# Weight conversion steps at the banks ahead of the seven-product pairs of a fused retention and two-MLP kernel: one per bank in place of two

## The chip, the cores and the metric

The kernel runs on one core of one Trainium2 chip. The metric is the device time of one execution in microseconds (us), the median of several runs. Engines are named as in the profile: PE is the matrix engine, DVE the vector engine, ACT the scalar engine, POOL and SP the two that here mostly issue transfers.

## The reference, cut to what matters

```python
def _attn_ref(q, k, v, lam):              # B=2, H=8, S=768, D=64; block 64
    ...                                   # decayed (retention) attention, a running 64x64 state per head
def _moe_ref(x, w_in, w_out):
    h = np.maximum(x @ w_in, 0.0)         # 512 -> 2048
    return (h * h @ w_out)                # 2048 -> 512
def _moe2_ref(x, w_in, w_out):
    h = x @ w_in
    g = np.maximum(0.01 * h, h)
    return (g @ w_out)
def reference(**kwargs):
    attn_out = _attn_ref(**attn_kwargs)
    x = attn_out.transpose(0, 2, 1, 3).reshape(B * S, H * D)   # 1536 x 512
    return _moe2_ref(_moe_ref(x))
```

The four weight matrices arrive as 64-bit words.

## The kernel before

First comes the retention (`retention`, one chunk of 128 tokens at a time), then two MLP layers. An MLP layer is cut into four stages by slices of 512 of the 2048 hidden columns; a stage is written (layer, slice), so the order is (0,0) ... (0,3), (1,0) ... (1,3). The 1536 tokens are three tiles of 512 (t = 0, 1, 2). In a stage, `first` multiplies the tokens by the slice of the first matrix: four banks (m = 0 to 3) a tile, each 12 matmuls of 128x512 in two halves of 6, and each half ends with a `yield`. `second` multiplies by the slice of the second matrix, again four banks of 12 matmuls. Values are split into a high and a low part, so one product takes three matmuls.

In stages (0,1) and (0,2), the set `seven`, tiles 0 and 1 of the second multiplication are done together by seven products in place of eight (`second_pair`, a Strassen form). Each of the 14 products (two output halves, p = 0 and 1) is 6 matmuls. They need sums of activations and sums of weights. `activate_for_seven` forms the former right behind each bank of `first`: for each half it chains L491 (a difference on DVE), L68 (a copy on ACT), L69 (the low part on DVE, T1), L449 to L451 (three more differences) and L69 again (T2), all with raised priority. The order of the products is P1 (A11 B11), S1 T1, A12 B21, S4 B22, S2 T2, A22 T4, then `first` of tile 2, then S3 T3.

The weights of later stages are prepared meanwhile. A piece is named (layer, slice, n, half), n = 0 for the first matrix and 1 for the second. `converting` is a generator that turns one piece of 64-bit words into floats and splits it; each `yield` is one step: L115, L116, L118, L121, L122 (then `fetch` issues the load of a later piece), L125, and, once the tile it goes to is open, L135 on ACT with L137 on DVE. L114 on ACT comes ahead of L115. A second-matrix piece of the `seven` stages has three more steps with the weight sums (`weight_sums`: L437 and L438; L439 and L440; L441 on ACT and L442). `convert` takes the next step of the oldest unfinished piece, at most two (of some kinds four) being open. The loop at the end of the kernel calls `convert` once behind every `yield` that is not False.

The order on PE is that of the program. On DVE, ACT, SP and POOL a scheduler sets the order ahead of time: where several instructions are ready, the one emitted earlier in the program goes first (L490, L495 and the like raise some by 400 places). So a call of `convert` sets where its step is emitted, which is a precedence and not a time. Working buffers limit how far ahead a piece can get: two for the raw words (`raw`), two for `hb` (pieces that `apart` names have their own), and one for `rb`, which L121 to L125 use and, for the pieces of `seven`, L437 to L442 in a tile of its own.

The steps of the prediction touch `first` (L505 to L525), `convert` (L153), `converting` (L98), `second_pair` (L620), and `keep` (L610), which copies a finished product (L612, ACT) to one of nine `f` tiles and writes it out from SP (partials) or adds it in memory from POOL (L616).

Of the kernel before, what the change touches and what calls it, by code (L numbers as in the profile page):

```python
# [19 lines left out]
def tile_retention_then_two_mlps(  # L20
# [37 lines left out]
    def bank():  # L58
        return psum.tile([P, 512], F32, tag="ps", name="ps")

    def plain():
        return fp.tile([P, TT], F32, tag="f", name="f")
# [110 lines left out]
    seven = {(0, 1), (0, 2)}  # L173
# [250 lines left out]
    def new_g(t, first_stage=False):  # L424
        if first_stage and t == 2:
            tags = ("sw0", "sw1")
        else:
            tags = (f"g{t % 2}h", f"g{t % 2}l")
        g[t] = [late.tile([P, KF, TT], F32R, tag=tag, name=tag) for tag in tags]
# [36 lines left out]
    def activate(l, src, r, ghi, glo):  # L466
        if l == 0:
            nc.scalar.activation(r, src, AF.Relu)
            nc.scalar.square(ghi, r)
            nc.scalar.square(r, r)  # L470
        else:
            nc.scalar.activation(ghi, src, AF.Prelu, alpha=0.01)
            nc.scalar.activation(r, src, AF.Prelu, alpha=0.01)
        nc.vector.tensor_tensor(out=glo, in0=r, in1=ghi, op=ALU.subtract)  # L474
# [4 lines left out]
    def activate_for_seven(t, m, src):  # L479
        r = plain()  # L480
        later[t, m] = r
        nc.scalar.activation(r, src, AF.Relu)
        ghi, glo = g[t]
        if (t, m % 2) != (1, 0):
            nc.scalar.square(ghi[:, m], r)
        nc.scalar.square(r, r)
        if (t, m % 2) != (1, 0):
            nc.vector.tensor_tensor(out=glo[:, m], in0=r, in1=ghi[:, m], op=ALU.subtract)
        if (t, m % 2) == (1, 0):
            with tc.high_priority(offset=400):  # L490
                nc.vector.tensor_tensor(out=later[0, m], in0=r, in1=later[0, m], op=ALU.subtract)  # L491
                split(ghi[:, m], glo[:, m], later[0, m])
        if (t, m % 2) == (1, 1):
            h = m // 2
            with tc.high_priority(offset=400):  # L495
                four_sums(later[0, m - 1], later[1, m - 1], later[1, m], later[0, m], False)
                if h == 0:
                    tt[2] = late.tile([P, 2, 2, TT], F32R, tag="t4", name="t4")
                split(tt[2][:, 0, h], tt[2][:, 1, h], later[1, m])

    def three(ps, ops, start, stop, again=False):
        for n, (a, b) in enumerate(ops):
            nc.tensor.matmul(ps, a, b, start=start and n == 0, stop=stop and n == len(ops) - 1, skip_group_check=again)  # L503

    def first(l, s, t, ms=range(KF)):  # L505
        for m in ms:
            if m == 0:
                new_g(t, (l, s) == (0, 0))
            ghi, glo = g[t]
            hi, lo = wts[l, s, 0, m // 2]  # L510
            cs = slice(m % 2 * P, (m % 2 + 1) * P)
            ps = bank()
            ops = []
            for kk in range(KD):
                ops += [(hi[:, kk, cs], xhi[t][:, kk]), (hi[:, kk, cs], xlo[t][:, kk]), (lo[:, kk, cs], xhi[t][:, kk])]
            three(ps, ops[:6], True, False)
            yield True
            three(ps, ops[6:], False, True)
            if (l, s) in seven and t < 2:
                activate_for_seven(t, m, ps)  # L520
            else:
                activate(l, ps, plain(), ghi[:, m], glo[:, m])
            if t == 2 and m % 2:
                opened.add((*stages[stages.index((l, s)) + 1], 0, m // 2) if (l, s) != stages[-1] else None)
            yield True  # L525


    def first_pair(s):
# [81 lines left out]
    def keep(src, dst, first):  # L610
        f = plain()
        nc.scalar.copy(f, src)  # L612
        if first:
            dma(dst, f)
        else:
            nc.gpsimd.dma_start(dst, f, accum_op=ALU.add)  # L616
# [3 lines left out]
    def second_pair(s):  # L620
# [53 lines left out]
        for p in both:  # L674
            keep(product(p, "D", "A22", "T4"), kept(p, 1, 0), False)
            yield True
        yield from first(0, s, 2)
        for p in both:
            keep(product(p, "B", "S3", "T3", False), partial[p]["P67"], True)
# [53 lines left out]
    def stage(l, s):  # L733
        if (l, s) == (0, 0):
            parts = [first(l, s, t, range(2)) for t in range(NTILE)]
            parts += [first(l, s, t, range(2, 4)) for t in (0, 2, 1)]
            return parts + [second(l, s, t) for t in (2, 0, 1)]
        if l == 0:
            parts = [first(l, s, t, ms) for ms in (range(2), range(2, 4)) for t in range(2)]
        else:  # L740
            parts = [first_pair(s)]
        if (l, s) in seven:
            return parts + [second_pair(s), second(l, s, 2)]
        if (l, s) == (0, NS - 1):
            return parts + [second(l, s, 0), second(l, s, 1, (0, 2, 1)), first(l, s, 2), second(l, s, 1, (3,)),
                            second(l, s, 2)]
        return parts + [second(l, s, 0), first(l, s, 2), second(l, s, 1), second(l, s, 2)]
# [36 lines left out]
```

## Time and profile before

| what | value |
|---|---|
| median of 3 runs | 577.12 us (576.59 to 578.66) |
| the profiled execution | 577.1 us, of which the span of its instructions is 575.3 us |
| PE busy | 566.2 us, 98% of the span |
| DVE busy | 413.8 us, 72% |
| ACT busy | 303.7 us, 53% |
| POOL busy | 103.3 us, 18% |
| mean granted clock of PE | 0.994 |

A row of the profile gives a line of the kernel, the engine and the operation, what it writes and reads, and its duration. "Idle before" is the time for which the engine had nothing to run just ahead of it, with what ended that time. PE busy is a weak measure, since matmuls overlap: one takes 0.39 us from start to end, and the next begins 0.23 us after it. So stalls on PE are read from the waits and the starts.

### The profile page before, as it was taken

Reading aid. Unit: us, or ns where it says so; the run is one execution under the profiler, and the core shown is the slowest. Engines: PE = TensorE matmul, PEld = TensorE weight load, DVE = VectorE, ACT = ScalarE, POOL = GpSimd, SP = SyncE. Lnnn points to the kernel's source line nnn. Section 1 sums busy time; section 2 is a strip of 40 time slices with the busy share of each in tenths; the row PEclk is TensorE's granted clock in tenths of the full one; section 3 lists DMA queues with packets and bytes.
Section 4 is the critical chain, followed back from the end, with each engine's and each line's share of the span. In section 5 each row is a group of like instructions: output and inputs, shape, how many; then the busy total and the mean of one; then the engine's idle time right before and its main releaser. Section 6 shows DMA issues by size and latency. Waiting matters only on the chain.

```text
span 575.3 us, 8060 instructions
## 1 busy us (share of the span) xinstructions
PE 566.2 (98%) x3075; PEld 472.8 (82%) x3075; DVE 413.8 (72%) x579; ACT 303.7 (53%) x477; POOL 103.3 (18%) x115
## 2 busy tenths in 40 slices
PE   7999999999999999999999999999999999999997
PEld 6888888888788888888888888888888888888886
DVE  3588999999927599498478999929782996217222
ACT  2344598556757587757448375453562376225110
POOL 3659100000044503433000000000213010210000
PEclk9899999999999999999999999999999999999999
DMA  8998434665498957999513215341529423651432
GB/s 173 235 218 177 142 130 140 221 190 186 171 157 137 161 168 176 214 254 188 174 38 91 81 34 216 129 164 73 110 49 246 108 32 43 78 87 56 164 111 91
DMA packets 79350, 80.75 MB, mean 140 GB/s; under 512 B 40264, under 2 KB 51792, under 8 KB 79312
## 3 DMA queue, kind: packets, MB, share of 16 engines
q1 hardware_dynamic: 61312, 62.15, 35.2%
q0 software_dynamic: 17472, 17.83, 22.9%
q8 instruction: 24, 0.39, 0.3%
q10 hardware_dynamic: 528, 0.26, 0.2%
q14 instruction: 14, 0.11, 0.1%
HBM read 55.05 MB, written 30.42 MB: 149 GB/s over the span
## 4 chain that ended last, share of the span: by engine, by line
PE 79%; DVE 10%; DMA 5%; issue 3%; ACT 2%; POOL 1%; SPq 0%; ACTq 0%; POOLq 0%; DVEq 0%
PE ps L503 72%; DMA raw<-in_moe_w_in 4%; PE ps L294 2%; DMA raw<-in_moe_w_out 2%; DVE hb L118 2%; PE ps L311 1%; DVE rb L122 1%; DVE hb L125 1%; PE ps L362 1%; DVE hb L115 1%; DVE rb L121 1%; PE ps L335 1%; ACT hb L114 1%; PE ps L220 1%; PE ps L360 1%
## 5 line engine op out<-in xcount | busy, mean ns | idle before, releaser
L503 PE MATMUL ps<-xhi,w1h 128*128 128x512 f32 x288 | 112.2, 389 | 0.0
L503 PE MATMUL ps<-xhi,w1l 128*128 128x512 f32 x288 | 112.0, 389 | 0.0
L503 PE MATMUL ps<-xlo,w1h 128*128 128x512 f32 x288 | 112.0, 389 | 0.0
L616 POOL DMA_DIRECT2D spill<-f x48 | 47.1, 1194 | 348.3 <-ACT f L612 348.2
L612 ACT COPY f<-ps 128x512 f32<-128x512 f32 x84 | 48.4, 585 | 69.6 <-PE ps L503 68.8
L503 PEld LDWEIGHTS ps<-xhi,w1l 128*128 128x128 f32 x288 | 54.1, 188 | 11.3
L503 PEld LDWEIGHTS ps<-xlo,w1h 128*128 128x128 f32 x288 | 54.1, 188 | 11.3
L503 PEld LDWEIGHTS ps<-xhi,w1h 128*128 128x128 f32 x288 | 54.0, 188 | 11.3 <-issue 0.2
L474 DVE TENSOR_TENSOR g0l<-f,g0h 128x512 fp32r<-128x512 f32 x52 | 35.1, 687 | 32.5 <-ACT f L470 20.9
L503 PE MATMUL ps<-w2l,g0h 128*128 128x512 f32 (+1 forms) x132 | 50.5, 383 | 0.0
L503 PE MATMUL ps<-w2h,g0l 128*128 128x512 f32 (+1 forms) x132 | 50.5, 383 | 0.0
L503 PE MATMUL ps<-w2h,g0h 128*128 128x512 f32 (+1 forms) x132 | 50.5, 383 | 0.0
L114 ACT ACTIVATE hb<-raw 128x1024 f32<-128x1024 f32 x32 | 36.8, 1149 | 21.5 <-DVE w2l L137 8.3
L137 DVE TENSOR_TENSOR w2l<-hb,w2h 128x1024 fp32r<-128x1024 f32 x16 | 19.5, 1222 | 39.8 <-ACT w2h L135 39.8
L503 PE MATMUL ps<-g0h,w2h 128*128 128x512 f32 x104 | 40.5, 389 | 0.0
L503 PE MATMUL ps<-g0l,w2h 128*128 128x512 f32 x104 | 40.5, 389 | 0.0
L503 PE MATMUL ps<-g0h,w2l 128*128 128x512 f32 x104 | 40.5, 389 | 0.0
L122 DVE SCALAR_TENSOR_TENSOR rb<-raw,rb 128x1024 f32<-128x1024 uint32 x32 | 39.4, 1231 | 0.4
L125 DVE TENSOR_TENSOR hb<-hb,rb 128x1024 f32<-128x1024 f32 x32 | 39.4, 1231 | 0.4
L118 DVE SCALAR_TENSOR_TENSOR hb<-raw,hb 128x1024 uint32<-128x1024 uint32 x32 | 39.1, 1221 | 0.3
L567 DVE TENSOR_TENSOR f<-ps,f 128x512 f32<-128x512 f32 x40 | 26.2, 684 | 9.9 <-PE ps L503 9.9
L716 DVE TENSOR_TENSOR f<-ps,f 128x512 f32<-128x512 f32 (+1 forms) x25 | 16.7, 668 | 22.9 <-PE ps L503 22.8
(143 smaller groups left out, 1155.0 us busy)
## 6 DMA issues: line engine op xcount, KB each, us to landing
raw<-in_moe_w_in SPq DMA_DIRECT2D x16, 1024.0 KB, 5.7
raw<-in_moe_w_out SPq DMA_DIRECT2D x16, 1024.0 KB, 5.1
spill<-f POOLq DMA_DIRECT2D x48, 256.0 KB, 5.5
spill<-f SPq DMA_DIRECT2D x24, 256.0 KB, 2.8
f<-spill SPq DMA_DIRECT2D x24, 256.0 KB, 3.0
k<-in_k SPq DMA_DIRECT2D x12, 256.0 KB, 5.0
q<-in_q SPq DMA_DIRECT2D x12, 256.0 KB, 5.1
v<-in_v SPq DMA_DIRECT2D x12, 256.0 KB, 5.3
```

The source lines that it names most:

```text
L114: nc.scalar.activation(hf, w_hi.bitcast(F32), AF.Abs)
L118: yield ve.scalar_tensor_tensor(out=hb, in0=w_hi, scalar=0xC0000000, in1=hb, op0=ALU.bitwise_and, op1=ALU.bitwise_or)
L122: yield ve.scalar_tensor_tensor(out=rf, in0=w_lo, scalar=2.0 ** -52, in1=rf, op0=ALU.mult, op1=ALU.mult)
L125: yield ve.tensor_tensor(out=hf, in0=hf, in1=rf, op=ALU.add)
L137: yield ve.tensor_tensor(out=lo, in0=hf, in1=hi, op=ALU.subtract)
L294: nc.tensor.transpose(ps[:, p, :], src[:, 2 * p:2 * p + 2, :].rearrange("s h d -> s (h d)"), ident)
L474: nc.vector.tensor_tensor(out=glo, in0=r, in1=ghi, op=ALU.subtract)
L503: nc.tensor.matmul(ps, a, b, start=start and n == 0, stop=stop and n == len(ops) - 1, skip_group_check=again)
L567: ve.tensor_tensor(out=out, in0=ps[h, where], in1=other, op=ALU.add)
L612: nc.scalar.copy(f, src)
L616: nc.gpsimd.dma_start(dst, f, accum_op=ALU.add)
L716: nc.vector.tensor_tensor(out=a, in0=ps, in1=a, op=ALU.add)
```

## The change

The second `yield` of each bank in `first` gives False in stages (0,1) and (0,2) for tiles 0 and 1, so the loop doesn't call `convert` there. All other calls stay.

```diff
@@ -522,7 +522,7 @@
                 activate(l, ps, plain(), ghi[:, m], glo[:, m])
             if t == 2 and m % 2:
                 opened.add((*stages[stages.index((l, s)) + 1], 0, m // 2) if (l, s) != stages[-1] else None)
-            yield True
+            yield (l, s) not in seven or t == 2
```

## Rows read from the trace of the kernel before

**Rows 1.** PE's granted clock in 40 equal slices, in tenths of full speed.

```profile
PEclk9899999999999999999999999999999999999999
```

**Rows 2.** Waits of PE over the whole span: us in total, times, longest.

```profile
PE ps L335 <- POOL qS L304: 2.4, 1, 2.4
PE ps L220 <- POOL pw L225: 1.5, 1, 1.5
PE ps L503 <- DVE g1l L69: 0.9, 1, 0.9
PE ps L311 <- ACT qT L298: 0.4, 2, 0.2
```

**Rows 3.** End of the chain that ended last: start us, us, what.

```profile
155.74 415.73 PE ps L503 x1844
```

**Rows 4.** Busy us of PE, PEld, DVE, ACT, POOL in one stretch, then PEclk and DMA.

```profile
129.00:151.00 22.00, 22.00 (x98) 18.21 (x97) 21.70 (x27) 15.54 (x25) 0.00 (x0) 1.00 0.48 163
```

**Rows 5.** Timeline of PE: first matmul of (0,1), P1, S1 T1, the wait, (0,2).

```profile
129.01 0.39 PE L503 MATMUL ps<-xhi,w1h 128*128 128x512 f32 x1
...
150.77 0.39 PE L503 MATMUL ps<-g0h,w2h 128*128 128x512 f32 x1
...
153.49 0.39 PE L503 MATMUL ps<-g1h,sw 128*128 128x512 f32 x1
...
155.74 0.50 PE L503 MATMUL ps<-g1l,sw 128*128 128x512 f32 x1 [0.92 <-DVE g1l L69]
...
193.07 0.39 PE L503 MATMUL ps<-xhi,w1h 128*128 128x512 f32 x1
```

**Rows 6.** Timeline of DVE, 123 to 137 us: steps of pieces, then the first activation.

```profile
123.51 1.23 DVE L442 TENSOR_TENSOR sw<-rb,sw 128x1024 fp32r<-128x1024 f32 x1 [1.11 <-ACT sw L441]
...
131.98 2.35 DVE L137 TENSOR_TENSOR w2l<-hb,w2h 128x1024 fp32r<-128x1024 f32 x2
...
136.23 0.69 DVE L488 TENSOR_TENSOR g0l<-f,g0h 128x512 fp32r<-128x512 f32 x1 [0.16 <-ACT f L486]
```

**Rows 7.** Timeline of DVE, 147 to 154 us, ahead of the wait of PE.

```profile
147.05 0.69 DVE L121 TENSOR_SCALAR rb<-hb 128x1024 uint32<-128x1024 uint32 x1
...
150.06 1.22 DVE L122 SCALAR_TENSOR_TENSOR rb<-raw,rb 128x1024 f32<-128x1024 uint32 x1
...
151.80 1.22 DVE L125 TENSOR_TENSOR hb<-hb,rb 128x1024 f32<-128x1024 f32 x1
152.93 0.69 DVE L491 TENSOR_TENSOR f<-f 128x512 f32<-128x512 f32 x1
153.53 0.42 DVE L437 TENSOR_TENSOR rb<-hb 128x256 f32<-128x256 f32 x1
```

**Rows 8.** Timeline of DVE, 173 to 193 us: idle ahead of it, L442, L137.

```profile
173.47 0.69 DVE L474 TENSOR_TENSOR g0l<-f,g0h 128x512 fp32r<-128x512 f32 x1 [11.10 <-ACT f L470]
...
184.27 1.22 DVE L442 TENSOR_TENSOR sw<-rb,sw 128x1024 fp32r<-128x1024 f32 x1 [0.73 <-ACT sw L441]
...
192.77 1.22 DVE L137 TENSOR_TENSOR w2l<-hb,w2h 128x1024 fp32r<-128x1024 f32 x1 [3.34 <-ACT w2h L135]
```

**Rows 9.** Timeline of SP's queue, 205 to 219 us: a load of raw words, a partial's write.

```profile
205.72 12.29 SPq L65 DMA_DIRECT2D raw<-in_moe_w_out  x2
218.74 0.34 SPq L65 DMA_DIRECT2D partial20P<-f  x1
```

**Rows 10.** Timeline of ACT, 224 us: a copy of a product.

```profile
224.15 0.59 ACT L612 COPY f<-ps 128x512 f32<-128x512 f32 x1 [0.71 <-DMA partial20P<-f]
```

**Rows 11.** Timeline of DVE: L122 of piece (0,3,0,1), and the low parts of T4.

```profile
216.34 1.22 DVE L122 SCALAR_TENSOR_TENSOR rb<-raw,rb 128x1024 f32<-128x1024 uint32 x1
...
225.84 1.29 DVE L69 TENSOR_TENSOR g0l<-f,g0h 128x512 fp32r<-128x512 f32 x2
```

**Rows 12.** Timeline of POOL: additions in memory, with DVE idle and with DVE busy.

```profile
162.34 2.74 POOL L616 DMA_DIRECT2D spill<-f  x3 [0.23 <-ACT f L612]
...
220.50 0.86 POOL L616 DMA_DIRECT2D spill<-f  x1 [23.59 <-ACT f L612]
```

## The prediction

> **What bounds the kernel now.** I read the waits of PE first, then the end of the chain, then the stages by windows, and last the timelines of DVE and SP. The whole span holds four kinds of wait on PE: three in the retention at the start, 4.3 us together, and one of 0.92 us behind them, on a low part of an activation (g1l, L69) [rows 2]. The chain says the same: from 155.74 us on it is matmuls alone, 1844 of them in 415.73 us, 0.225 us each [rows 3]. PE's granted clock is at its upper level, 2.4 GHz, in every slice but the second [rows 1], 1.00 in (0,1) [rows 4]. So behind the retention PE has one gap, and what can be won there is 0.92 us, 0.16% of the time. What can be lost has no such limit: DVE is near full in stage (0,1)'s first eight banks, 21.70 of 22.00 us [rows 4].
>
> **What the change takes away, adds and moves.** No instruction is added or removed; 8 of the 46 calls of `convert` in stage (0,1) are left out, and 8 in (0,2), so steps are emitted later. I counted the calls by hand through the generators. Of the 46 calls of (0,1), 8 found every open piece blocked and 38 emitted a step; the 38 calls that are left emit a step each. By the second bank of `second` of tile 0 in (0,3) the queue has caught up, and from there on both programs emit the same steps at the same places.
>
> For the times, half a bank or a product is 6 matmuls. Eight banks are 16 halves: P1 starts at 150.77 and the stage at 129.01, so 21.76 / 16 = 1.36 us each [rows 5]. With that:
> - Piece (0,1,1,1), needed in this very stage: its last sum step is emitted with the 7th half before (129.01 + 7 x 1.36 = 138.5 us), with the 13th after (146.7). It ran at 123.51 [rows 6], and S1 T1 needs it at 153.49 [rows 5].
> - Piece (0,2,1,0), L137: 14th half (148.1) before, 22nd after (with the wait, 159.9). It ran in the pair of L137 that starts at 131.98 [rows 6].
> - Piece (0,2,1,1), L125: 33rd half (174.8) before, 45th after (191.1). It ran at 151.80 [rows 7].
>
> So the steps already run 15 to 23 us ahead of the place where they are emitted. What holds them is not emission but buffers: SP's load of the next raw words sits 12.29 us in its queue, and the sums of (0,2,1,0), whose first instruction ran at 153.53, end at 184.27 [rows 7 to 9]. Emission then only decides between instructions that are ready together. The first activation reaches DVE at 136.23 [rows 6]. The steps that ran before it had no activation to give way to, and those that ran after it, from (0,2,0,0)'s last on, were emitted behind all eight banks (after 150.8) even in the program of before. They fill DVE's gaps already as the last in precedence, and being later still changes nothing there. I therefore cost the change at **0**, between two bounds: -0.92 us (the one wait goes) and, were the steps held at their new places, what the third rival gives.
>
> What hides it: the gap of 11.10 us that DVE has ahead of 173.47 [rows 8]. Eight steps, between 0.69 and 1.22 us each [rows 7], are 5.5 to 9.8 us and fit. Even if every step ran only where it is now emitted, the pieces would be in time: (0,1,1,1)'s sums at about 146.7 + 1.23 and a copy on ACT, some 149, against 153.49; (0,2,1,1) opens at 192.77 in any case [rows 8] and is needed at 193.07 + 21.76 = 214.8 us [rows 5]. If that cover goes, each us of lateness is a us of PE.
>
> The loads (`fetch`) move with L122, past SP's other transfers; they start when a raw buffer comes free, which L122 sets, so they stay where L122 stays. POOL's additions don't move.
>
> **The rivals.**
>
> *Nothing moves* (my forecast): 577.1 us, as profiled; the profiled run stands at the median of 577.12, so nothing is to be shifted.
>
> *The wait goes.* One pair does swap precedence while both are ready. The sums of (0,2,1,0) are emitted with the 39th half in both programs, but (0,2,1,1)'s L118 to L125 come ahead of that before and behind it after. If the sums get the single `rb` first, L121, L122 and L125 (0.69 + 1.22 + 1.22 = 3.1 us) leave the stretch from 147.05 to 153.0, where they stand ahead of L491 and so of the g1l that PE waits for [rows 7]. The wait was 0.92 us: 577.1 - 0.92 = **576.2**. Against it: the two may get `rb` in the order in which the pieces were opened, which the change leaves as it is, and ACT, which feeds L491, would come next. The sums would then hold `rb` up to 184.27, and (0,2,1,1) would end some 4 us later than that, still far from 214.8.
>
> *SP's queue* (slower). Place: stage (0,2), where the second of two loads of raw words waits until L122 of (0,3,0,1) frees its buffer, and P1's write, 218.74, stands behind it [rows 9]. The `f` tiles that these writes free are scarce: a copy on ACT at 224.15 waited 0.71 us for that very write [rows 10], and behind it in ACT's queue are the copies for T4, which A22 T4 needs at 193.07 + 26 x 1.36 = 228.4. That L122 ran at 216.34 [rows 11] and is now emitted with the 29th half, not the 21st: 8 x 1.36 = 10.9 us later. If it follows its emission, the write, the copy and T4 come 10.9 us later. T4's low part was done at 225.84 + 1.29 = 227.1 [rows 11], 1.3 us early, so PE would lose 10.9 - 1.3 = 9.6 us: **586.7**. It decides against the kernel (over 0.5%, 2.9 us) once that L122 is more than 4.2 us late. Against it: the L122 ran when its load had landed and DVE had room, 5 us ahead of its emission (193.07 + 21 x 1.36 = 221.6), and nothing ready on DVE lies between its old and its new place; and SP's order is made by the same scheduler, which puts the write first if it sees the buffer come free late.
>
> *POOL held up by DVE.* Additions issued from POOL take 2.74 / 3 = 0.91 us each with DVE idle and 0.86 with DVE at work [rows 12]: no hindrance is seen. The Trainium skill (SBUF — State Buffer, "SBUF: two separate sides") says that descriptors of transfers from POOL can't be written while DVE runs an instruction that holds the port the two share, and it speaks against putting conversion steps into the pair. The trace doesn't bear that out. As a mechanism of this kernel: six additions, each kept for one L121 of 0.69 us, come 4.1 us late, and less T4's margin of 1.3 us PE loses 2.8 us: **579.9**.
>
> **How the numbers follow.** Nothing moves: 0.60. The wait goes, in whole or part: 0.27. A small new wait that I don't see, under 2.9 us: 0.04. SP's queue: 0.06. POOL: 0.02. Something outside these, faster: 0.01. The predicted time is that of the first, **577.1 us**. Within 0.5%, about what a measurement of this kernel can tell from no change, lie the first three: 0.91. Slower by more: 0.08. Faster by more: 0.01, since 2.9 us aren't there to be won: PE's gap behind the retention is 0.92 us. The range goes from 576.2 less some 0.4 us of the scatter of the runs (576.59 to 578.66) to the upper end of that scatter with a little room for a small wait: 575.8 to 579.0. It leaves out the two slower rivals, 0.08.
>
> **What would show it.** Right: DVE's steps between 136 and 155 us in nearly the order of before, L442 of (0,1,1,1) near 123.5, one wait of PE of 0 to 0.9 us near 155, and the 1844 matmuls of the end in about 415.7 us. The second case shows as L437 ahead of (0,2,1,1)'s L121 and no wait at S1 T1. The third shows as P1's write later than 220 in SP's queue and a wait of PE at A22 T4 near 228. My forecast is wrong if DVE's order between 129 and 155 differs widely, that is, if emission weighs more than the buffers do, or if PE waits anywhere behind 156 us.

## The result, and the profile after

The changed kernel takes **580.91 us** (median, 579.16 to 582.29) against 576.19 us (575.53 to 578.66) for the kernel before, timed side by side: ratio 1.0075, 95% interval 1.0048 to 1.0102. It is slower by 4.7 us, where no change was forecast. The profiled execution took 580.36 us, with a span of 578.6 us against 575.3 us before.

First the waits of PE over the whole span of the changed kernel (us in total, times, longest), which answer to [rows 2]:

```profile
PE ps L503 <- ACT g1h L68: 3.0, 1, 3.0
...
PE ps L503 <- DVE g1l L69: 0.7, 1, 0.7
```

These two rows of L503 are the ones behind the retention. The end of the chain, which answers to [rows 3], says where the second of them lies:

```profile
219.96 354.77 PE ps L503 x1568
```

The matmuls without a gap begin at 219.96 and no longer at 155.74. So the wait in stage (0,1) is gone and a larger one stands in (0,2). PE's timeline, which answers to [rows 5], gives the lengths of the stages and the gap (first matmuls of (0,1) and (0,2); the third to fifth matmul of S1 T1 and a later one; the first of (0,3)):

```profile
127.92 0.39 PE L503 MATMUL ps<-xhi,w1h 128*128 128x512 f32 x1
190.48 0.39 PE L503 MATMUL ps<-xhi,w1h 128*128 128x512 f32 x1
...
215.41 0.39 PE L503 MATMUL ps<-g1h,sw 128*128 128x512 f32 x1
218.81 0.50 PE L503 MATMUL ps<-g1h,sw 128*128 128x512 f32 x1 [3.00 <-ACT g1h L68]
219.96 0.50 PE L503 MATMUL ps<-g1l,sw 128*128 128x512 f32 x1 [0.65 <-DVE g1l L69]
...
223.67 0.42 PE L503 MATMUL ps<-g0l,w2h 128*128 128x512 f32 x1
...
258.88 0.39 PE L503 MATMUL ps<-xhi,w1h 128*128 128x512 f32 x1
```

| | before, us | after, us |
|---|---|---|
| first matmul of (0,0) | 63.59 | 62.51 |
| first matmul of (0,1) | 129.01 | 127.92 |
| length of (0,1) | 64.06 | 62.56 |
| length of (0,2) | 62.56 | 68.40 |

The retention of this execution ended 1.09 us earlier by chance: no call ahead of (0,1) is changed, and over the fourteen profiles (0,0) begins anywhere from 62.51 to 63.62 us. Stage (0,1) is 1.50 us shorter, stage (0,2) 5.84 us longer: -1.09 - 1.50 + 5.84 = +3.25 us, the difference of the spans (578.6 - 575.3). Without the part of chance it is +4.34 us, which stands to the 4.7 us of the medians.

The 5.84 us come in two parts. From 215.41 to 219.96 two matmuls' time, 0.45 us, became 4.55: 4.10 us lost to two waits. Then PE ran slowly. Its windows (us; busy and count of PE, PEld, DVE, ACT, POOL; granted clock, DMA share, GB/s):

```profile
216.00:218.00 2.00, 0.00 (x0) 0.00 (x0) 2.00 (x3) 1.52 (x3) 0.00 (x0) 1.00 0.00 0
...
220.00:222.00 2.00, 2.00 (x6) 1.57 (x7) 2.00 (x3) 0.83 (x2) 0.19 (x1) 0.58 0.69 258
222.00:224.00 2.00, 2.00 (x7) 1.57 (x6) 1.99 (x4) 1.13 (x2) 0.67 (x1) 0.57 0.57 57
```

Behind 3.40 us in which no matmul began, and a second wait of 0.65 us, the granted clock is 0.58 and 0.57, near its lower level of 1.2 GHz. Nine matmuls from 219.96 to 223.67 take 3.71 us, where 9 x 0.2266 = 2.04 is usual (96 in the 21.76 us of eight banks): 1.67 us. 4.10 + 1.67 = 5.77 of the 5.84 us.

**Where the gap comes from** is read backwards. DVE's timeline of (0,1) comes first; it answers to [rows 7, 8]:

```profile
142.56 0.42 DVE L437 TENSOR_TENSOR rb<-hb 128x256 f32<-128x256 f32 x1
...
147.18 0.42 DVE L440 TENSOR_TENSOR rb<-hb,rb 128x256 f32<-128x256 f32 x1
147.52 1.22 DVE L118 SCALAR_TENSOR_TENSOR hb<-raw,hb 128x1024 uint32<-128x1024 uint32 x1
...
170.88 0.69 DVE L474 TENSOR_TENSOR g0l<-f,g0h 128x512 fp32r<-128x512 f32 x1 [11.41 <-ACT f L470]
...
181.52 1.23 DVE L442 TENSOR_TENSOR sw<-rb,sw 128x1024 fp32r<-128x1024 f32 x1 [0.73 <-ACT sw L441]
182.78 0.69 DVE L121 TENSOR_SCALAR rb<-hb 128x1024 uint32<-128x1024 uint32 x1
183.51 1.23 DVE L122 SCALAR_TENSOR_TENSOR rb<-raw,rb 128x1024 f32<-128x1024 uint32 x1
184.77 1.22 DVE L125 TENSOR_TENSOR hb<-hb,rb 128x1024 f32<-128x1024 f32 x1
```

The exchange over the single `rb` has happened: the sums of (0,2,1,0) take it at 142.56, hold it until L442 ends at 182.75, and L121 to L125 of (0,2,1,1) run at 182.78 to 186.0 and no longer at 147.05 to 153.0 [rows 7]. That is what frees S1 T1 of (0,1) from its wait. It also moves L122 from 150.06 to 183.51, and L122 is the last reader of a raw buffer. SP's queue shows what stands behind it, the loads of (0,3,0,0) and (0,3,0,1):

```profile
184.76 0.38 SPq L65 DMA_DIRECT2D raw<-in_moe_w_in  x1
...
200.40 0.38 SPq L65 DMA_DIRECT2D raw<-in_moe_w_in  x1
```

In the kernel before the first one was issued at 151.35 us, as SP's queue there has it:

```profile
151.35 0.38 SPq L65 DMA_DIRECT2D raw<-in_moe_w_in  x1
```

So the load of (0,3,0,0) is 33 us later. In the kernel before, the piece's L114 ran at 176.78 and its L115 to L118 at 177.93 to 180.62, in stage (0,1); now they come in (0,2), ahead of the L122 whose end lets the load of (0,3,0,1) start. DVE's gap of 11 us, the cover that was counted on, is idle in both kernels (11.10 and 11.41 us): L121 to L125 of (0,2,1,1) can't use it, since the sums hold `rb` right through it. ACT's two L114 in the kernel before:

```profile
176.78 1.12 ACT L114 ACTIVATE hb<-raw 128x1024 f32<-128x1024 f32 x1
...
207.42 1.12 ACT L114 ACTIVATE hb<-raw 128x1024 f32<-128x1024 f32 x1 [1.64 <-DMA raw<-in_moe_w_in]
```

ACT's timeline in (0,2) of the changed kernel shows the cost:

```profile
191.25 1.12 ACT L114 ACTIVATE hb<-raw 128x1024 f32<-128x1024 f32 x1 [1.10 <-DMA raw<-in_moe_w_in]
...
204.87 0.64 ACT L486 ACTIVATE f<-f 128x512 f32<-128x512 f32 x1
209.09 1.12 ACT L114 ACTIVATE hb<-raw 128x1024 f32<-128x1024 f32 x1 [3.59 <-DMA raw<-in_moe_w_in]
210.12 0.58 ACT L482 ACTIVATE f<-ps 128x512 f32<-128x512 f32 x1
...
211.39 0.63 ACT L486 ACTIVATE f<-f 128x512 f32<-128x512 f32 x1
...
218.13 0.62 ACT L68 CAST g1h<-f 128x512 fp32r<-128x512 f32 x1 [0.58 <-DVE f L491]
```

ACT stood 3.59 us at L114 of (0,3,0,1), for its load (1.64 us before). Counted from the start of the stage, this load is issued at 9.92 us in place of 7.32 and takes 8.69 us to its reader in place of 7.03: 2.60 + 1.66 = 4.26 us. The chain that ended last passes through both loads (start us, us, what):

```profile
183.51 1.24 DVE rb L122
184.76 6.47 DMA raw<-in_moe_w_in
191.25 1.13 ACT hb L114
...
199.11 1.24 DVE rb L122
...
200.40 8.67 DMA raw<-in_moe_w_in
209.09 0.02 ACT hb L114
```

The activations L482 to L486, which start right behind L114 without a wait of their own, came late. DVE stands for them in turn and then has more steps of weights to work off (L115 and L116 of (0,3,0,1) had run by then in the kernel before):

```profile
208.42 0.68 DVE L450 TENSOR_TENSOR f<-f 128x512 f32<-128x512 f32 x1
212.06 0.69 DVE L488 TENSOR_TENSOR g0l<-f,g0h 128x512 fp32r<-128x512 f32 x1 [2.96 <-ACT f L486]
...
217.41 0.69 DVE L491 TENSOR_TENSOR f<-f 128x512 f32<-128x512 f32 x1
...
219.22 0.69 DVE L69 TENSOR_TENSOR g1l<-f,g1h 128x512 fp32r<-128x512 f32 x1
```

The same operations in the kernel before, and PE's first matmul that reads this g1l:

```profile
210.99 0.69 DVE L450 TENSOR_TENSOR f<-f 128x512 f32<-128x512 f32 x1
211.59 0.68 DVE L488 TENSOR_TENSOR g0l<-f,g0h 128x512 fp32r<-128x512 f32 x1
...
215.74 0.69 DVE L491 TENSOR_TENSOR f<-f 128x512 f32<-128x512 f32 x1
...
217.48 0.69 DVE L69 TENSOR_TENSOR g1l<-f,g1h 128x512 fp32r<-128x512 f32 x1
...
218.45 0.39 PE L503 MATMUL ps<-g1l,sw 128*128 128x512 f32 x1
```

Counted from the start of the stage (193.07 before, 190.48 after), L450 is at 17.92 and 17.94: not late. L488 is at 18.52 and 21.58: 3.06 us late, by ACT's stand. L491 is at 22.67 and 26.93: 4.26 us late, 1.20 more, since seven operations in place of five lie between the two. And the margin that might have taken it up was small: before, this g1l was done at 217.48 + 0.69 = 218.17 and read at 218.45, **0.28 us** to spare. 4.33 us of lateness at L69 less 0.28 is 4.05, and PE lost 4.10.

### The profile page after: what moved, and what is told of

It is laid out like the page before. It is cut to its first block, busy times and chain, and to the rows that moved or that the text cites. A ratio compares the mean times of both kernels' runs of the same rounds, so it can differ in the third digit from the quotient of the medians.

```text
span 578.6 us, 8054 instructions
## 1 busy us (share of the span) xinstructions
PE 565.7 (98%) x3075; PEld 472.1 (82%) x3075; DVE 414.6 (72%) x579; ACT 305.4 (53%) x477; POOL 104.5 (18%) x115
## 4 chain that ended last, share of the span: by engine, by line
PE 86%; DMA 5%; DVE 3%; issue 2%; SPq 1%; ACT 1%; POOL 0%; POOLq 0%; ACTq 0%
PE ps L503 81%; DMA raw<-in_moe_w_in 4%; PE ps L311 1%; PE ps L362 1%; SPq L65 1%; PE ps L360 1%; PE ps L294 1%; DMA k<-in_k 1%; PE ps L335 1%; DVE rb L122 0%; DVE rb L121 0%; DVE hb L116 0%; DVE hb L115 0%; DVE pw L240 0%; DVE hb L118 0%
## 5 line engine op out<-in xcount | busy, mean ns | idle before, releaser
L616 POOL DMA_DIRECT2D spill<-f x48 | 48.9, 1237 | 351.1 <-ACT f L612 351.1
L503 PE MATMUL ps<-xhi,w1h 128*128 128x512 f32 x288 | 112.3, 390 | 0.0
L503 PE MATMUL ps<-xlo,w1h 128*128 128x512 f32 x288 | 112.2, 389 | 0.0
L503 PE MATMUL ps<-xhi,w1l 128*128 128x512 f32 x288 | 112.2, 389 | 0.0
L503 PEld LDWEIGHTS ps<-xhi,w1h 128*128 128x128 f32 x288 | 54.1, 188 | 11.4 <-issue 0.2
L503 PEld LDWEIGHTS ps<-xhi,w1l 128*128 128x128 f32 x288 | 54.1, 188 | 11.2
L503 PEld LDWEIGHTS ps<-xlo,w1h 128*128 128x128 f32 x288 | 54.1, 188 | 11.1
L503 PE MATMUL ps<-w2l,g0h 128*128 128x512 f32 (+1 forms) x132 | 50.6, 383 | 0.0
L503 PE MATMUL ps<-w2h,g0l 128*128 128x512 f32 (+1 forms) x132 | 50.6, 383 | 0.0
L503 PE MATMUL ps<-w2h,g0h 128*128 128x512 f32 (+1 forms) x132 | 50.5, 383 | 0.0
L114 ACT ACTIVATE hb<-raw 128x1024 f32<-128x1024 f32 x32 | 37.0, 1155 | 22.2 <-DMA raw<-in_moe_w_in 9.4
L137 DVE TENSOR_TENSOR w2l<-hb,w2h 128x1024 fp32r<-128x1024 f32 x16 | 19.5, 1223 | 36.7 <-ACT w2h L135 36.7
L503 PE MATMUL ps<-g0h,w2h 128*128 128x512 f32 x104 | 40.7, 392 | 0.0
L503 PE MATMUL ps<-g0l,w2h 128*128 128x512 f32 x104 | 40.6, 390 | 0.0
L503 PE MATMUL ps<-g0h,w2l 128*128 128x512 f32 x104 | 40.5, 389 | 0.0
L122 DVE SCALAR_TENSOR_TENSOR rb<-raw,rb 128x1024 f32<-128x1024 uint32 x32 | 39.4, 1232 | 0.5
L125 DVE TENSOR_TENSOR hb<-hb,rb 128x1024 f32<-128x1024 f32 x32 | 39.4, 1232 | 0.4
L118 DVE SCALAR_TENSOR_TENSOR hb<-raw,hb 128x1024 uint32<-128x1024 uint32 x32 | 39.0, 1220 | 0.3
```

The source lines that it names most:

```text
L114: nc.scalar.activation(hf, w_hi.bitcast(F32), AF.Abs)
L118: yield ve.scalar_tensor_tensor(out=hb, in0=w_hi, scalar=0xC0000000, in1=hb, op0=ALU.bitwise_and, op1=ALU.bitwise_or)
L122: yield ve.scalar_tensor_tensor(out=rf, in0=w_lo, scalar=2.0 ** -52, in1=rf, op0=ALU.mult, op1=ALU.mult)
L125: yield ve.tensor_tensor(out=hf, in0=hf, in1=rf, op=ALU.add)
L137: yield ve.tensor_tensor(out=lo, in0=hf, in1=hi, op=ALU.subtract)
```

## The experiments

Theory A was formed from this reading: the late load alone costs, through ACT and DVE in (0,2), and the exchange over `rb` in (0,1) is its cause; the rate of steps and the second stage of the change do nothing. The first four kernels take the change apart.

**The first stage alone.**

```diff
-            yield (l, s) not in seven or t == 2
+            yield (l, s) != (0, 1) or t == 2
```

> The change in stage (0,1) alone; (0,2) emits two steps per bank as before. Theory A (the sums of piece (0,2,1,0) take the single rb ahead of (0,2,1,1) in stage (0,1), hold it to about 182 us, and so push the load of (0,3,0,0) from 151 to 185 us and three of its DVE steps into the first banks of (0,2)): all of the loss comes from this part, so 580 to 581.5 us, with a wait of PE of 3 us or more at S1 T1 of (0,2) and none in (0,1). Theory B (the loss comes from the steps that (0,2) itself emits later): the (0,1) wait goes and nothing else, 574.5 to 575.5 us.

Measured: 582.09 us, ratio 1.0086 (1.0058 to 1.0114). The load is issued at 185.62, and here it took 11.5 us to its end; ACT's row:

```profile
197.11 1.12 ACT L114 ACTIVATE hb<-raw 128x1024 f32<-128x1024 f32 x1 [6.11 <-DMA raw<-in_moe_w_in]
```

PE waits 3.2, 1.1 and 0.4 us in (0,2), which is 71.18 us long; (0,1) is 62.56. The half of the change in (0,1) brings all of its cost, though that cost falls in (0,2). The time is 0.6 us above the bound of theory A.

**The second stage alone.**

```diff
-            yield (l, s) not in seven or t == 2
+            yield (l, s) != (0, 2) or t == 2
```

> The change in stage (0,2) alone. Theory A: the time of before, 576 us plus or minus 0.6, with the one wait of PE near 155 us and no wait in (0,2). Theory B: 578 to 582 us, with a wait in (0,2).

Measured: 576.67 us, ratio 1.0001 (0.9985 to 1.0017); one wait of PE, 0.6 us in (0,1), the load at 149.81, (0,2) 62.56 us long. The eight calls left out in (0,2) change nothing that can be told from noise. Where the cost comes from is as theory A has it in both runs.

**The sums opened earlier, at the old rate.** In the kernel before, the sums of (0,2) may begin ahead of `first` of tile 2 and not behind S3 T3:

```diff
-        yield from first(0, s, 2)
+        opened.add(("sums", 0, 2)); yield from first(0, s, 2)
```

> The kernel before, two steps per bank, with one edit: the weight sums of stage (0,2) are opened ahead of first of tile 2 in (0,1) and not behind S3 T3, so that the sums of (0,2,1,0) are emitted ahead of (0,2,1,1)'s L118 to L125. Theory A (it is that one swap over rb, not the rate of steps): 579.5 to 581.5 us, L437 near 143 us, the load of (0,3,0,0) near 185 us, and waits of PE of 3 us or more in (0,2). Theory B (the rate of steps): the time of before, 575.5 to 576.8 us.

Measured: 581.89 us, ratio 1.0091 (1.0064 to 1.0118). L437 runs at 143.82, ahead of L118 (148.77), L121 and L122 (183.68); the load is issued at 184.93; ACT stands 0.76 and 3.03 us at L114; (0,2) is 68.33 us long. PE waits 1.8 and 1.8 us in (0,2), and 0.4 us in (0,1). With two steps per bank as before, the exchange alone makes the loss (0.4 us above the forecast's bound). What the change touches is the order in which two users of `rb` are emitted.

**A scratch tile for each.** In the changed kernel the sums of the second pair get a tile of their own, in the place of one that is used only later; all work is done:

```diff
-            rb = cv.tile([P, 4 * CW], U32, tag="rb", name="rb")
+            rb = (late if s == 2 else cv).tile([P, 4 * CW], U32, tag="sw0" if s == 2 else "rb", name="rb")
```

> The changed kernel, with the weight sums of stage (0,2) working in a tile of their own (the memory of sw0) in place of rb; nothing is left out. Theory A: rb isn't held, the load of (0,3,0,0) goes back to about 150 us and the waits of PE in (0,2) go; in (0,1) a wait of 0 to 1.5 us may come or go with DVE's order there. 574.5 to 576.8 us. Theory B: 579.5 us or more, as the steps are emitted just as late as in the changed kernel.

Measured: 575.72 us, ratio 0.9986 (0.9957 to 1.0016). The load is issued at 151.53 and the end of the chain has no gap of PE behind the retention:

```profile
63.45 506.57 PE ps L503 x2244
```

With the exchange undone the loss is gone, at the lower rate. That the exchange is the cause is thus shown from both sides. The next five kernels ask by which link the late load costs.

**Three steps fewer on DVE.** The changed kernel without L115, L116 and L118 of (0,3,0,0), the steps that the late load pushes from DVE's gap into (0,2):

```diff
+        if key == (0, 3, 0, 0):
+            yield True
+            yield True
+            yield True
+        else:
         ...
```

> The changed kernel without L115, L116 and L118 for piece (0,3,0,0) (0.7 + 0.7 + 1.2 us of DVE; that piece's weights are not converted rightly). In the changed kernel they stand on DVE ahead of L122 of (0,3,1,0), which frees the raw buffer for the load of (0,3,0,1), issued 9.9 us into stage (0,2) in place of 7.3; ACT then stands at L114 of (0,3,0,1) for 3.6 us until it has landed. Theory A1 (those three steps are what delays the load and so ACT): the load is issued some 7.4 us into (0,2), ACT's wait at L114 is 0 to 2 us, the waits of PE in (0,2) fall from 3.65 us to under 1; 575 to 577.5 us. Theory A2 (DVE is simply full in (0,2) or the transfers are slow there, wherever these steps stand): waits of PE of 2.5 us or more, 579 us or more.

Measured: 581.93 us, ratio 1.0096 (1.0066 to 1.0125); PE waits 2.6, 0.9, 0.7 and 0.2 us; ACT stood 5.08 us for the load of (0,3,0,0) and 1.82 for the next; (0,2) is 69.66 us long. Leaving these steps out brings nothing here. But the load of (0,3,0,0) took 10.4 us to its reader (6.5 in the changed kernel), and that of (0,3,0,1) was issued 12.7 us into (0,2), where theory A1 wanted 7.4. So the steps aren't the whole of the cost, and what they add was not measured by itself.

**ACT not waiting for one load, and for neither.** L114 of (0,3,0,1), and then L114 of both pieces, reads a tile that has long been there (the line as it stands in the first kernel; in the second the condition is `key[:3] == (0, 3, 0)`):

```diff
-        nc.scalar.activation(hf, w_hi.bitcast(F32), AF.Abs)
+        nc.scalar.activation(hf, xhi[2].rearrange("p k f -> p (k f)")[:, 0:4 * CW].bitcast(F32) if key == (0, 3, 0, 1) else w_hi.bitcast(F32), AF.Abs)
```

> The changed kernel with L114 of piece (0,3,0,1) reading a token tile that is long there in place of the raw words (that piece's weights are not converted rightly), so that ACT has no load to wait for; DVE's steps on the piece still wait for it. Theory A3 (ACT standing at L114 is the link by which the late load reaches PE): ACT's wait is gone and the waits of PE in (0,2) fall to under 1.5 us; 575 to 578 us. Rival (DVE's order and load in (0,2) are the link): waits of PE stay at 3 us or more, 579.5 us or more.

Measured: 580.91 us, ratio 1.0062 (1.0003 to 1.012). The runs scatter widely (576.33 to 582.81), so the time decides little. In the profile ACT now stood 3.90 us at L114 of the other piece, whose load took 9.3 us here, PE waits 1.7 and 0.7 us, and (0,2) is 67.05 us long. The stand at (0,3,0,1) was taken away, but the one at (0,3,0,0) grew: the run doesn't decide between theory A3 and its rival. The next kernel takes both stands away.

> The changed kernel, with L114 of both pieces (0,3,0,0) and (0,3,0,1) reading a tile that has long been in memory in place of the raw words. What it leaves out: the true high parts of these two pieces, so the numbers of slice 3 are not the reference's. The order and the loads stay as in the changed kernel; only ACT no longer stands at L114 for them. Theory A-C (the late loads cost because ACT, which works in order, stands at L114 with the copies of activations behind it): ACT's stands at L114 in (0,2) shrink from 1.1 to 3.9 us each to under 0.5, PE waits under 1 us in sum behind the retention, stage (0,2) is under 63.8 us long, and the time is 576 to 577.5. DVE still reads the raw words at L122, so a wait could sit there instead. Rival D (the wait is not ACT's; it is DVE that stands at L115 to L122 or is crowded by the late steps, with L491 and L69 behind them): PE still waits 2 us or more at S1 T1 of (0,2), stage (0,2) over 66 us, time 580 or more.

Measured: 577.34 us, ratio 1.003 (1.0004 to 1.0056), within the bounds of theory A-C for the time; but the stage, 64.57 us, and the waits of PE, 0.9 + 0.6, are above them. The load was as late (187.01) and slow (9.3 us to its end) as elsewhere. Waits of all engines between 195 and 222 us (us in total, times, longest):

```profile
DVE hb L118 <- DMA raw<-in_moe_w_in: 3.0, 1, 3.0
...
PE ps L503 <- ACT g1h L68: 0.9, 1, 0.9
PE ps L503 <- DVE g1l L69: 0.6, 1, 0.6
```

Of the loss of 0.75% some 0.45 went with ACT's stands (1.0075 against 1.003; as the two intervals touch, the share is rough). DVE now waits 3.0 us for the same load at L118, and some 2 us in (0,2) remain; that this wait makes them is read from the row, not tested.

**Without the additions.** In the changed kernel, and then in the kernel before, the ten additions of POOL behind the products of (0,1) are left out:

```diff
-        for p in both:
+        for p in both if s != 1 else ():
             p1, p6, p67 = (partial[p][n] for n in ("P1", "P6", "P67"))
```

> The changed kernel without the ten additions in memory that POOL issues from L686 at the end of stage (0,1) (so the partial products of that stage are not added). The load of (0,3,0,1) took 8.6 us to land at about 200 us, among these transfers. Theory C (contention of transfers is what makes ACT wait): it lands in about 5.5 us, ACT's wait at L114 falls from 3.6 to under 1 us and PE's waits in (0,2) to under 1 us; 575 to 577.5 us. Theory A1 (the load is issued too late by 2.6 us): the landing may be shorter, but PE still waits 1 us or more in (0,2); 577.5 to 581 us.

Measured: 576.29 us, ratio 1.0009 (0.9987 to 1.0031). The load is late here too (185.72), ACT stands only 1.44 and 0.31 us for the two, PE waits 0.6 us, and (0,2) is 63.81 us long. The first 4 us from the issue of the load of (0,3,0,1), in this kernel:

```profile
201.44:205.44 4.00, 4.00 (x19) 3.34 (x18) 4.00 (x6) 2.26 (x4) 0.00 (x0) 1.00 0.69 205
```

and in the changed kernel with its additions:

```profile
200.40:204.40 4.00, 4.00 (x19) 3.30 (x19) 4.00 (x6) 2.26 (x4) 0.00 (x0) 1.00 1.18 187
```

The DMA engines' share is 0.69 against 1.18, while they moved 205 against 187 GB/s. From its issue to the start of L114 that load took 206.86 - 201.44 = 5.4 us here and 209.09 - 200.40 = 8.7 us there. For the load of (0,3,0,0) the pair shows no such difference (6.8 and 6.5 us).

> The kernel before, without the ten additions in memory that POOL issues behind the products of stage (0,1) (L686). What it leaves out: these additions, so tiles 0 and 1 miss a part of slice 1. It is the control to the changed kernel without them, which took 576.29. Theory C (the additions cost only through the late loads that land among them): nothing changes, 576 to 577, within 0.3% of before, and the one wait of under 1 us in (0,1) stays. Rival E (the additions cost several us in every order, by some other way, so that taking them away shortens any kernel): 573 or less.

Measured: 576.0 us, ratio 0.9991 (0.9973 to 1.0008). In the order of before the additions cost nothing that shows in the time, although the load of (0,3,0,1) took 5.5 us at most without them (ACT didn't stand for it) and 7.0 with them. Theory C holds for the time: the loss needs both, the late load and the additions beside it. In the profiles the late load without the additions still makes (0,2) 1.25 us longer (63.81 against 62.56), which is hidden behind what (0,1) gained.

**The late load alone.** In the kernel before, the load of (0,3,0,0) is emitted behind the sums of (0,2,1,0), and a small operation on DVE that reads these sums writes into the raw buffer ahead of it, so that it can't start earlier; all work is done:

```diff
-    def fetch():
+    def fetch(late=None):
...
-            r = raw.tile([P, 4 * CW], I64, tag="raw", name="raw")
+            r = raw.tile([P, 4 * CW], I64, tag="raw", name="raw"); late is not None and nc.vector.tensor_tensor(out=r.bitcast(F32)[:, 0:P], in0=late[:, 0, 0, 0], in1=late[:, 1, 0, 0], op=ALU.add)
...
-        if begun_mlp:
+        if begun_mlp and key != (0, 2, 1, 1):
             fetch()
...
-            yield from weight_sums(key, f"t{h + 2}", blocks, rb.bitcast(F32))
+            yield from weight_sums(key, f"t{h + 2}", blocks, rb.bitcast(F32)); key == (0, 2, 1, 0) and fetch(sums[key])
```

> The kernel before, with two steps per bank as it was, in which only the load of (0,3,0,0) is made late: it is emitted behind the sums of (0,2,1,0), and a small DVE operation of 128x128 that reads the second half of these sums writes into the raw buffer first, so the load can't start before L442 at about 184 us (151.35 in the kernel before). Nothing is left out of the computation. DVE's order in stage (0,1) up to that L442 is that of before, with L121 to L125 of (0,2,1,1) ahead of the sums. Theory A-C (the late load is what costs, by ACT standing at L114 in (0,2)): the load is issued at about 185, ACT stands at L114 of (0,3,0,0) and (0,3,0,1) for 3 us or more together, PE waits 2 us or more at S1 T1 of (0,2), that stage is 66 to 69 us long, (0,1) keeps its one wait of about 0.9 us, and the time is 580 to 583. Rival G (the cost comes from another part of the exchange, as the later L121 to L125 of (0,2,1,1) or the earlier sums): with these at their old places (0,2) is 62.6 to 63.5 us long and the time 576 to 577.5.

Measured: 580.47 us, ratio 1.0068 (1.0049 to 1.0087). L121 of (0,2,1,1) runs at 146.54 and L122 at 149.55, at their old places; the load and ACT's waits:

```profile
185.17 0.38 SPq L65 DMA_DIRECT2D raw<-in_moe_w_in  x1
...
190.77 1.13 ACT L114 ACTIVATE hb<-raw 128x1024 f32<-128x1024 f32 x1 [2.59 <-DMA raw<-in_moe_w_in]
...
209.18 1.16 ACT L114 ACTIVATE hb<-raw 128x1024 f32<-128x1024 f32 x1 [1.91 <-DMA raw<-in_moe_w_in]
...
218.92 0.50 PE L503 MATMUL ps<-g1h,sw 128*128 128x512 f32 x1 [1.04 <-ACT g1h L68]
220.08 0.50 PE L503 MATMUL ps<-g1l,sw 128*128 128x512 f32 x1 [0.65 <-DVE g1l L69]
```

Stage (0,1) keeps its wait (0.9 us, 63.96 us long) and (0,2) is 66.44 us long, as theory A-C expects (PE's waits there, 1.7 us as shown, are a little under the 2 expected). The load alone, with nothing exchanged, is enough, in a kernel that does all its work. Rival G falls.

**The two rates with a scratch tile each.** To see whether a version beats both kernels, the scratch tile of its own was timed longer in the changed kernel, and put into the kernel before by the same edit.

> The changed kernel with a scratch tile for the sums of the second seven-product stage of their own, in the place of a tile that is used only later; nothing is left out. A longer comparison of the version that had no wait of PE behind the retention. If the one wait of before is worth 1.5 us (as stage (0,1) of 64.06 against 62.56 us says), the ratio to before is 0.9974, 574.9 to 575.7; if it is worth nothing, 1.000.

Measured: 575.78 us, ratio 0.9992 (0.9973 to 1.0011). The interval holds 1.000 and, at its edge, 0.9974, so the 1.5 us of the wait are not seen and not quite ruled out. In this profile, of the same kernel as above, ACT stood 3.64 us for (0,3,0,1), and PE waited 0.8 and 0.6 us in (0,2), 64.48 us long; the first profile had 1.99 us and no wait.

> The kernel before, with two steps per bank as it was, and the scratch tile of the sums of the second seven-product stage of their own, as in the run beside it; nothing is left out. Theory A (the changed rate matters only through who gets the one scratch tile): with a tile for each, both rates are equal within 0.3%, and the steps of (0,2,1,1) run at 147 to 152 us in both. Whether the wait at S1 T1 of (0,1) stays here (L121 to L125 ahead of L491, 0.9 us, and then 576 to 577) or goes as in the run beside it (575) shows what the lower rate is worth by itself: 0 to 1.5 us. Rival F (the rate itself costs): the run beside it is slower than this one by 1.5 us or more.

Measured: 575.76 us, ratio 0.9985 (0.9967 to 1.0002); no wait of PE behind the retention. The two rates are equal, rival F falls, and neither version can be told from the kernel before. The wait was not worth 1.5 us in every execution: where the order of before was kept, it was 0.92, 0.91, 0.57 and 0.34 us long in four profiles, with (0,1) at 64.06, 63.96, 63.43 and 63.19 us against 62.56 without a wait.

All profiles together:

| kernel | load of (0,3,0,0) issued, us | ACT standing for both loads, us | (0,2), us |
|---|---|---|---|
| second stage alone | 149.81 | 1.04 | 62.56 |
| before | 151.35 | 1.64 | 62.56 |
| before, no additions | 149.88 | 0.00 | 62.56 |
| before, scratch of its own | 151.04 | 1.69 | 62.58 |
| changed, scratch of its own | 151.53 | 1.99 | 62.80 |
| the same, second profile | 151.83 | 3.64 | 64.48 |
| changed, no additions | 185.72 | 1.75 | 63.81 |
| ACT waiting for neither load | 187.01 | 0.00 | 64.57 |
| ACT waiting for one load | 185.36 | 3.90 | 67.05 |
| sums opened earlier | 184.93 | 3.79 | 68.33 |
| late load alone | 185.17 | 4.50 | 66.44 |
| **changed** | 184.76 | 4.69 | 68.40 |
| first stage alone | 185.62 | 6.39 | 71.18 |
| changed, three steps fewer | 185.44 | 6.90 | 69.66 |

By and large the stage grows with ACT's stand, though not row by row (3.79 us with 68.33, 4.50 with 66.44); with the load early, up to some 2 us of it are free.

How long the late load takes to its reader goes with its place among POOL's additions. In the changed kernel, with the sums opened earlier and with the late load alone, it is issued 0.02 to 0.80 us ahead of the second addition into a partial (L686, partial11P, at 184.78 in the changed kernel); it takes 5.6 to 6.5 us, and POOL then waits 4.6 to 4.9 us for the first addition to end. In the four other kernels that have the late load and the additions it is issued 0.9 to 2.4 us behind that addition; it takes 9.3 to 11.5 us, and POOL waits 1.6 to 2.1 us. These are seven profiles without an exception, but no run sets this order on purpose.

## Why the prediction was wrong

**The change at 0 ("nothing moves").** Wrong. The argument was that steps run far ahead of the places where they are emitted, so that emission decides only between instructions that are ready together. That holds, as the second stage alone shows (1.0001). But one pair was ready together, the text had found it, and it gave it 0.27. The reason against it, that the two get `rb` in the order in which the pieces were opened, was a guess: with the sums opened earlier and nothing else changed, the order turned (L437 at 143.82).

**"The wait goes".** Its mechanism happened to the letter: L437 ahead of L121, no wait at S1 T1 of (0,1). Its gain was put too low for the profile that it was read from: 0.92 us by the row of the wait, 1.50 by the length of the stage. The wait as shown is only part of the gap in PE's starts.

**The step that failed** is the cost of 0 for steps that move ("being later still changes nothing there"), together with the loads that "stay where L122 stays". L122 of (0,2,1,1) didn't stay: it went from 150.06 to 183.51. The rival that had the exchange priced it no better, in its last sentence: (0,2,1,1) "would end some 4 us later than that, still far from 214.8". It asks when the piece itself is needed, and the piece was in time (L125 ended at 186.0). It doesn't ask what L121 to L125 release: the loads were not moved with L122. Followed through: L122 at 183.5, load at 184.8, the first steps of (0,3,0,0) pushed into (0,2), two loads beside POOL's additions, ACT standing in order at L114, and 0.28 us of margin at S1 T1 of (0,2), which was not read. The price of this tail is +5.84 us in that profile; the sum of the rival would have been -1.50 + 5.84 = +4.34, some 581.4 from 577.1, and not 576.2.

**The cover.** The gap [rows 8] was costed as room for eight delayed steps. But the prediction's own rows have the sums of (0,2,1,0) in `rb` from 153.53 to 184.27 in the kernel before, all through the gap, and in the changed kernel they hold it from 142.56 to 182.75. Room on DVE is of use only to a step that has its buffer and its data: the displaced L121 to L125 had no `rb`, and the gap stayed idle in both kernels.

**A row misread.** The 12.29 us of [rows 9] are no time that one load sits in its queue: the row joins two loads, issued at 205.72 and 217.63. The price of the rival in SP's queue doesn't rest on it.

**The slower rivals.** SP's queue: the place was in (0,2) and the resource, a raw buffer freed by L122, was the right one, but the wrong L122, and the wrong sufferer: ACT's L114, not the write of a partial. What the text had against it came true: L122 of (0,3,0,1) did run late (221.03), and SP put the two writes (219.78 and 220.27) ahead of the second load (222.27). POOL held up by DVE: not what happened, as an addition of POOL in (0,2) takes 0.86 us here too. The additions into the partials did suffer beside the load: POOL waited 4.91 us for the one into partial10P (up to 192.04), against 1.59 us (up to 189.73) before.

**The range** ended at 579.0, worked out from the scatter and a small wait; the time was 580.91. Its last sign of being wrong, "if PE waits anywhere behind 156 us", named what came.

The Trainium skill (PSUM — Partial Sum Buffer, "Engine vs sequencer instructions") says that the queues of ScalarE, VectorE and GpSimdE are strict FIFO: L482 at 210.12, right behind L114 and with no wait of its own, agrees. The Trainium skill (DMA: Bandwidth & Descriptors, "Issuing engines are not separate DMA queues") says that transfers from SP and from POOL run on the same 16 engines and interleave: the 8.7 us against 5.4 us without the additions agree for the load of (0,3,0,1), while for (0,3,0,0) the pair of runs shows nothing.

**Open**: by what means the order of issue sets whether the load or the additions come first, and so whether the load takes 5.6 or 11.5 us; and what makes the 2 us that stay in (0,2) when ACT waits for neither load.

## What to carry to other kernels

Where two users of a single scratch buffer are ready together, a later emission of one can turn their order, and the price is not when the displaced steps are needed but what they release: follow each freed buffer to the load that it starts, to where that load lands, and to the in-order engine that stands for it. Read the margin of the next stage before calling a delay harmless; here it was 0.28 us at the same product whose wait was to be won. Price a stall on PE by what its stage grows, not by the number on its wait, and in more than one profile.

## What the runs showed of the hardware that was not expected

- A wait of PE shown as 0.92 us made its stage 1.50 us longer, at a granted clock of 1.00 throughout; waits of 0.91, 0.57 and 0.34 us in three other profiles made it 1.40, 0.87 and 0.63 us longer.
- Behind waits at S1 T1 of (0,2) the granted clock fell: 0.58 and 0.57 for 4 us in the changed kernel (waits of 3.00 and 0.65 us), 0.50 (1.2 GHz) from 223 to 227 us in the first stage alone. It also fell behind waits of 1.04 and 0.65 us with the late load alone (0.50 from 222 to 224 us), and stayed at 1.00 behind 0.85 and 0.59 us where ACT waited for neither load. In the changed kernel this added 1.67 us to a loss of 4.10.
- The same load of 1 MB reached its reader 5.6 to 11.5 us after its issue beside POOL's additions: 5.6 to 6.5 us when it was issued ahead of the second of them, 9.3 to 11.5 us when behind it.
